# Second layers by seven products of blocks instead of eight, 1024 rows at a time, in channel attention and two MLPs

## Chip, cores and metric

The kernel runs on one core of one Trainium2 chip. The metric is the time on the device in microseconds (us), the median of several runs. For the kernel before it is 1119.35 us, over three runs of 1117.44, 1119.35 and 1119.87 us.

## What is computed

Attention over channels makes a 256 x 256 matrix from q and k and applies it to v; its 6016 rows go through two MLPs of width 2048 one after the other. Cut to what matters:

```python
# q, k, v: 6016 x 256 in fp32; the weights arrive as 64-bit floats
s = (k / (norm(k, axis=1) + 1e-6)).T @ (q / (norm(q, axis=1) + 1e-6)) / tau   # 256 x 256
a = softmax(s)                       # along the last axis
x = v @ a                            # 6016 x 256
h = x @ moe_w_in                     # 6016 x 2048
g = moe_s * maximum(h, 0)**2 + moe_b
y = g @ moe_w_out                    # 6016 x 256
h = y @ moe2_w_in                    # 6016 x 2048
g = maximum(h, 0) + alpha * minimum(h, 0)       # alpha: 2048 values in 0..0.3
out = g @ moe2_w_out                 # 6016 x 256
```

## The kernel before

**Arithmetic.** Every fp32 factor of an MLP is split into a high part (`...h`, the value rounded to the matmul's fp32r type) and a low part (`...l`, what is left), and a product is made of three matmuls: high by high, low weight by high, high weight by low. The attention matrix is folded into the first weights: `w1 = a @ moe_w_in` (four groups `make_w1`, L496 to L509), so x is v itself, turned so that channels lie on partitions.

**Start.** For some 60 us q and k stream in; TensorE makes the score matrix, ACT and DVE the norms and the softmax. Meanwhile and afterwards weights arrive in 32 units of 512 KB and are turned from 64-bit floats into fp32 and split (`unit`): two passes on ACT, four on DVE, then a cast on ACT and a subtraction on DVE.

**Chunks and steps.** The rows are cut into 12 chunks (480, ten of 512, 416). A step `t` is one block of 128 hidden units of one chunk, so there are 12 x 16 = 192 steps. A step has four stages of six matmuls: `stage_a` makes the first MLP's hidden block in a PSUM bank `h1` (L520 to L523, function `hidden`), `stage_b` adds its share to the two output halves `y0`, `y1` (L590 to L592), `stage_c` (bank `h2`, L520 to L523) and `stage_d` (banks `o0`, `o1`, L664 to L666) do the same for the second MLP. `h1` and `h2` have two banks each; with the four for outputs these are the eight banks. Stage B is two steps behind A. The second MLP is a chunk behind the first (`SC = NF + SB`), so from the second chunk on all four stages alternate.

**Around the matmuls.** After stage A ACT makes relu and square (L558, L559), and DVE, in the first chunks ACT, the high part (L537 or L541) and DVE the low part (L542). After stage C ACT makes relu of h and of -h (L633, L634), DVE the multiply-add with alpha (L640) and both parts. At a chunk's end y gets its scale and bias on ACT and is split; the outputs are transposed on DVE (L678) and stored by eight DMAs on SP (L681). The next chunk's v is loaded by SP (`load_v`) and transposed and split by DVE.

**Order.** The instructions of each engine stand in the order in which the code issues them, by hand. A small clock per engine (`run`, `fill`, `PARTS`) decides where the parts of the weight units go between the steps. All DMAs are on SP's queue, except the first pieces of k on ACT's.

## Time and profile before

| | us |
|---|---|
| median of three runs | 1119.35 |
| profiled execution | 1118.72 |
| its span in the profile | 1116.9 |
| PE busy | 1098.7 |
| DVE busy | 740.5 |
| ACT busy | 553.8 |

The granted TensorE clock was 0.996 of full speed over the span. Matmuls overlap in the pipeline: a row of the timeline has a start and a duration, and the next one may start before the first has ended, so the distance between starts, not the duration, is what an instruction takes of its engine. A row ends, in brackets, with the idle time before it and what ended that.

### The profile page before, as it was taken

How to read it: one execution, taken by the hardware profiler on the slowest of the kernel's cores; microseconds unless marked ns; L12 is line 12 of the kernel's file. 1: busy time of each engine (PE TensorE's matmuls, PEld its weight loads, DVE VectorE, ACT ScalarE, POOL GpSimd, SP SyncE). 2: the span in 40 equal slices, each digit the busy share in tenths (PEclk: the TensorE clock that was granted, in tenths of full speed). 3: DMA queues.
4: the chain of work that ended last, by engine and by line, in shares of the span. 5: the costliest groups of instructions: out<-in, count | busy, mean ns of one | idle time of the engine just before them, and what ended most of it. 6: DMA issues, size and time to landing. Idle time of an engine off the chain costs nothing.

```text
span 1116.9 us, 13535 instructions
## 1 busy us (share of the span) xinstructions
PE 1098.7 (98%) x4898; PEld 917.0 (82%) x4898; DVE 740.5 (66%) x1284; ACT 553.8 (50%) x946; POOL 0.7 (0%) x6
## 2 busy tenths in 40 slices
...
PEclk9989999999999999999999999999999999999999
...
DMA packets 114627, 42.31 MB, mean 38 GB/s; under 512 B 102784, under 2 KB 103552, under 8 KB 114560
## 3 DMA queue, kind: packets, MB, share of 16 engines
q1 hardware_dynamic: 113696, 39.35, 14.6%
...
q8 instruction: 38, 0.62, 0.2%
...
## 4 chain that ended last, share of the span: by engine, by line
PE 89%; DVE 7%; DMA 2%; ACT 1%; issue 1%; ACTq 0%; DVEq 0%; SPq 0%
PE h L521 15%; PE h L523 15%; PE h L520 15%; PE o L666 8%; PE o L664 8%; PE o L665 7%; PE y L590 7%; PE y L591 7%; PE y L592 7%; DMA qk<-in_k_dram 2%; DVE acc L353 1%; PE wp L496 1%; DVE g1l L542 0%; DVE sq L340 0%; DVE wi L163 0%
## 5 line engine op out<-in xcount | busy, mean ns | idle before, releaser
L640 DVE SCALAR_TENSOR_TENSOR gc<-neg,nal_sb,gc 128x512 f32<-128x512 f32 (+2 forms) x192 | 141.6, 738 | 178.6 <-ACT neg L634 178.2
L633 ACT ACTIVATE gc<-h 128x512 f32<-128x512 f32 (+2 forms) x192 | 113.1, 589 | 257.7 <-PE h L523 243.1
L558 ACT ACTIVATE ga<-h 128x512 f32<-128x512 f32 (+2 forms) x192 | 113.1, 589 | 252.4 <-PE h L523 233.6
L520 PE MATMUL h<-xh,w1h 128*128 128x512 f32 (+2 forms) x384 | 150.8, 393 | 0.4 <-ACT w1h L505 0.4
L521 PE MATMUL h<-xh,w1l 128*128 128x512 f32 (+2 forms) x384 | 149.4, 389 | 0.2 <-DVE w1l L509 0.2
L590 PE MATMUL y<-g1h,wo1h 128*128 128x512 f32 (+2 forms) x384 | 148.2, 386 | 0.4 <-ACT wo1h L172 0.2
L521 PE MATMUL h<-yh,wi2l 128*128 128x512 f32 (+2 forms) x384 | 148.2, 386 | 0.2 <-DVE wi2l L174 0.2
L591 PE MATMUL y<-g1h,wo1l 128*128 128x512 f32 (+2 forms) x384 | 148.1, 386 | 0.2 <-DVE wo1l L174 0.2
L520 PE MATMUL h<-yh,wi2h 128*128 128x512 f32 (+2 forms) x384 | 147.9, 385 | 0.4 <-ACT wi2h L172 0.4
L592 PE MATMUL y<-g1l,wo1h 128*128 128x512 f32 (+2 forms) x384 | 148.0, 386 | 0.0
L664 PE MATMUL o<-g2h,wo 128*128 128x512 f32 (+2 forms) x368 | 142.7, 388 | 0.5 <-DVE g2h L541 0.5
L666 PE MATMUL o<-g2l,wo 128*128 128x512 f32 (+2 forms) x368 | 142.5, 387 | 0.0
L665 PE MATMUL o<-g2h,wo 128*128 128x512 f32 (+2 forms) x368 | 142.4, 387 | 0.0
L542 DVE TENSOR_TENSOR g1l<-ga,g1h 128x512 fp32r<-128x512 f32 (+2 forms) x192 | 130.7, 681 | 16.8 <-ACT g1h L537 1.9
L542 DVE TENSOR_TENSOR g2l<-gc,g2h 128x512 fp32r<-128x512 f32 (+2 forms) x184 | 126.2, 686 | 17.4 <-PE h L523 0.9
L541 DVE CAST g1h<-ga 128x512 fp32r<-128x512 f32 (+1 forms) x158 | 66.4, 420 | 87.1 <-ACT ga L559 86.0
L559 ACT ACTIVATE ga<-ga 128x512 f32<-128x512 f32 (+2 forms) x192 | 119.7, 623 | 6.1
L523 PE MATMUL h<-xl,w1h 128*128 128x512 f32 (+2 forms) x384 | 117.8, 388 | 0.0
L523 PE MATMUL h<-yl,wi2h 128*128 128x512 f32 (+2 forms) x384 | 116.7, 385 | 0.0
L634 ACT ACTIVATE neg<-h 128x512 f32<-128x512 f32 (+2 forms) x192 | 112.1, 584 | 0.1
L541 DVE CAST g2h<-gc 128x512 fp32r<-128x512 f32 (+2 forms) x184 | 77.9, 423 | 16.9 <-DVE gc L640 0.5
L521 PEld LDWEIGHTS h<-xh,w1l 128*128 128x128 f32 x384 | 72.8, 190 | 15.6 <-issue 1.0
(106 smaller groups left out, 1281.0 us busy)
## 6 DMA issues: line engine op xcount, KB each, us to landing
...
wi1r<-in_moe_w_in_dram SPq DMA_DIRECT2D x8, 512.0 KB, 7.5
wo1r<-in_moe_w_out_dram SPq DMA_DIRECT2D x8, 512.0 KB, 4.3
wi2r<-in_moe_w_in_dram SPq DMA_DIRECT2D x8, 512.0 KB, 3.6
wo2r<-in_moe_w_out_dram SPq DMA_DIRECT2D x8, 512.0 KB, 3.7
...
```

The source lines that it names most:

```text
L520: nc.tensor.matmul(pt[:, :n], wh[:, h, fs], xh, start=(h == 0), stop=False)
L521: nc.tensor.matmul(pt[:, :n], wl[:, h, fs], xh, start=False, stop=False)
L523: nc.tensor.matmul(pt[:, :n], wh[:, h, fs], xhl[h][1][:, :n], start=False, stop=(h == NC2 - 1))
L541: nc.vector.tensor_copy(hi[:, :n], g[:, :n])
L542: nc.vector.tensor_tensor(lo[:, :n], g[:, :n], hi[:, :n].bitcast(F32), ALU.subtract)
L590: nc.tensor.matmul(yp[:, :m], wo1h[:, f, cs], hi[:, :m], start=(f == 0), stop=False)
L591: nc.tensor.matmul(yp[:, :m], wo1l[:, f, cs], hi[:, :m], start=False, stop=False)
L592: nc.tensor.matmul(yp[:, :n], wo1h[:, f, cs], lo[:, :n], start=False, stop=(f == NF - 1))
L640: nc.vector.scalar_tensor_tensor(g[:, :n], neg[:, :n], nal_sb[:, f : f + 1], g[:, :n], op0=ALU.mult, op1=ALU.add,)
L664: nc.tensor.matmul(op, wo2[:, f, 0, cs], hi, start=(f == 0), stop=False)
L665: nc.tensor.matmul(op, wo2[:, f, 1, cs], hi, start=False, stop=False)
L666: nc.tensor.matmul(op, wo2[:, f, 0, cs], lo, start=False, stop=(f == NF - 1))
```

## The change

**Seven products.** Rows are taken 1024 at a time, as two halves: six chunks of 2 x 480, 2 x 512 (four) and 2 x 480 rows. The unit is now a *cycle* c, one pair of hidden blocks (256 units) of one chunk: 8 pairs x 6 chunks x 2 MLPs = 96 cycles. A cycle makes four hidden tiles by the first layer, as before with six matmuls each (`a_tile`, i: hidden block i % 2, half i // 2): B11, B21 of the first half, B12, B22 of the second. The second layer multiplies a 2 x 2 scheme of weight blocks (A) with these four by Strassen's scheme in Winograd's form: seven products, each of three matmuls into a bank of its own, P1 to P7, where the sum over the eight pairs is kept. Before, this took eight products. The sums of blocks on the data side, `T1 = B12 - B11`, `B12 = B22 - B12`, `B11 = B12 + B11`, `B21 = B21 - B11`, are made by DVE in fp32, then split into high and low parts G0 to G3 (`g_ops`); those on the weight side are made once for each unit. The seven banks are put together at the end of each chunk by additions on DVE (`results`). With seven banks for the products, one is left, `h`, for all hidden tiles.

**Order of the MLPs.** All six chunks go through the first MLP (cycles 0 to 47), then all through the second (48 to 95). The results of the first go to DRAM (`yd`) by DMAs on POOL's queue and are read back as the second's input, into a ring of three slots `xt`. The second MLP's weight units are converted and split during the first half, staged in DRAM (`wid`, `wod`) and read back into the first's places around cycles 40 to 48, on POOL's queue too.

**Steps of the activations.** In the first half ACT makes relu from the bank and then squares. In the second, ACT copies the tile out of the bank with a scale per partition of +1 or -1 (`sg_sb`, the sign folded into the weights), and DVE makes max(g * alpha, g) in one instruction (L700).

**Who sets the order.** A class `Plan` now collects all instructions behind the start with their engine, an estimated duration, and what they read and write, and sorts them by a list schedule: TensorE's order is as written, ACT's and DVE's go by the latest start time, and a cast may go to either engine. `LOOK` keeps ACT free shortly before a tile's bank is to be emptied (`boost` over 5).

```diff
-        chunks.append((n0, min(CH if n0 else CH - 32, N - n0)))
+    sizes = [480, 512, 512, 512, 512, 480]
+    firsts = [2 * sum(sizes[:j]) for j in range(len(sizes))]
+    NCHUNK = len(sizes)
...
-        bufs = 2 if tag in ("h1", "h2") else 1
-        return ps.tile([P, CH], F32, tag=tag, name=name, bufs=bufs)
+        return ps.tile([P, CH], F32, tag=tag, name=name)
...
+BACKLOG = (0.8, 3.0)
+LOOK = 0.2
...
+            for o in now:
+                us = o["us"][e] if isinstance(o["us"], dict) else o["us"]
+                if any(u["boost"] > 5 and u["r"] < t + us - look.get(e, 9.0) for u in soon):
+                    continue
+                pick = o
+                break
+            if pick is None:
...
+        parts += [
+            ("dve", est("tt", P), lambda: sub(S[:, 0, :], A21, A22, ALU.add), [kw], [ks]),
+            ("dve", est("tt", P), lambda: sub(S[:, 1, :], S[:, 0, :], A11, ALU.subtract), [kw], [ks]),
+            ("dve", est("tt", P), lambda: sub(S[:, 2, :], A11, A21, ALU.subtract), [kw], [ks]),
+            ("dve", est("tt", P), lambda: sub(S[:, 3, :], A12, S[:, 1, :], ALU.subtract), [kw], [ks]),
...
+        PROD = {
+            "P1": (0, 0, 0), "P2": (2, 0, 1), "P3": (6, 1, 0), "P5": (3, 2, 0),
+            "P7": (5, 2, 1), "P6": (4, 3, 0), "P4": (1, 3, 1),
+        }
...
+        def a_tile(c, i):
+            ph, j, p = c // 48, c // 8 % NCHUNK, c % 8
+            n = sizes[j]
+            f2, x = i % 2, i // 2
+            kx = (2 * (c // 8) + x) % 3
+            qq, f0 = p // 2, (p % 2) * 2 + f2
+            def go():
+                t = hb[c, i] = bank("h", f"h{c}_{i}")
+                w, xx = W["wA", qq], xt[kx]
+                fs = slice(f0 * P, (f0 + 1) * P)
+                for h in range(NC2):
+                    nc.tensor.matmul(t[:, :n], w[:, h, 0, fs], xx[:, h, 0, :n], start=(h == 0), stop=False)
+                    nc.tensor.matmul(t[:, :n], w[:, h, 1, fs], xx[:, h, 0, :n], start=False, stop=False)
+                for h in range(NC2):
+                    nc.tensor.matmul(t[:, :n], w[:, h, 0, fs], xx[:, h, 1, :n], start=False, stop=(h == NC2 - 1))
+            reads = [("x", kx, h, y) for h in range(2) for y in range(2)]
+            reads += [("wAh", qq, h) for h in range(2)] + [("wAl", qq, h) for h in range(2)]
+            op("pe", 6 * (0.0133 + n * 0.2134 / CH), go, reads, [("bank", "h")])
+            g = gA[c % 2][:, f2, :n] if x == 0 else gB[:, 1 + f2, :n]
+            kg = ("gA", c % 2, f2) if x == 0 else ("gB", 1 + f2)
+            if ph == 0:
+                op("act", est("act", n), lambda: nc.scalar.activation(g, hb.pop((c, i))[:, :n], AF.Relu),
+                   [("bank", "h")], [kg], boost=6.0)
+            else:
+                fc = 2 * p + f2
+                op("act", est("act", n), lambda: nc.scalar.activation(
+                    g, hb.pop((c, i))[:, :n], AF.Copy, scale=sg_sb[:, fc : fc + 1]),
...
+        def g_ops(c):
+            ph, j, p = c // 48, c // 8 % NCHUNK, c % 8
+            n = sizes[j]
+            a = gA[c % 2]
+            k11, k21, kt, k12, k22 = ("gA", c % 2, 0), ("gA", c % 2, 1), ("gB", 0), ("gB", 1), ("gB", 2)
+            V = nc.vector
+            B11, B21, T1, B12, B22 = a[:, 0, :n], a[:, 1, :n], *(gB[:, i, :n] for i in range(3))
+            if ph == 0:
+                op("act", est("act", 2 * n), lambda: nc.scalar.activation(
+                    a[:, :, :n], a[:, :, :n], AF.Square), [], [k11, k21])
+                for g, kk in ((B12, k12), (B22, k22)):
+                    op("act", est("act", n), lambda g=g: nc.scalar.activation(g, g, AF.Square), [], [kk])
+            else:
+                for f2, g, kk in ((0, B11, k11), (1, B21, k21), (0, B12, k12), (1, B22, k22)):
+                    al = al_sb[:, 2 * p + f2 : 2 * p + f2 + 1]
+                    op("dve", est("stt", n), lambda g=g, al=al: V.scalar_tensor_tensor(
+                        g, g, al, g, op0=ALU.mult, op1=ALU.max), [], [kk])
+            def hilo(k, src, keys):
+                m = len(keys)
+                hi, lo = (G[k][:, y, :m, :n] if m > 1 else G[k][:, y, 0, :n] for y in (0, 1))
+                kh = [("Gh", k, x) for x in range(m)]
+                kl = [("Gl", k, x) for x in range(m)]
+                op(either, HI(m * n), lambda e: copy(e, hi, src), keys, kh, leave=BACKLOG[ph])
+                op("dve", est("tt", m * n), lambda: V.tensor_tensor(
+                    lo, src, hi.bitcast(F32), ALU.subtract), keys + kh, kl)
+            tt = est("tt", n)
+            hilo(0, a[:, :, :n], [k11, k21])
+            op("dve", tt, lambda: V.tensor_tensor(T1, B12, B11, ALU.subtract), [k11, k12], [kt])
+            op("dve", tt, lambda: V.tensor_tensor(B12, B22, B12, ALU.subtract), [k22], [k12])
+            hilo(1, B22, [k22])
+            op("dve", tt, lambda: V.tensor_tensor(B11, B12, B11, ALU.add), [k12], [k11])
+            op("dve", tt, lambda: V.tensor_tensor(B21, B21, B11, ALU.subtract), [k11], [k21])
+            hilo(2, gB[:, 0:2, :n], [kt, k12])
+            hilo(3, a[:, :, :n], [k11, k21])
...
+        def b_mms(c):
+            j, p = c // 8 % NCHUNK, c % 8
+            n = sizes[j]
+            first, last = p == 0, p == NPAIR - 1
+            res = []
+            for tag, (wb, k, x) in PROD.items():
+                m = n + 2 if c < 8 and tag in ("P1", "P2", "P5") else n
+                for s in range(3):
+                    def go(tag=tag, wb=wb, k=k, x=x, s=s, m=m):
+                        if first and s == 0:
+                            acc_t[tag] = bank(tag, f"{tag}_{c}")
+                        w = W["wB", p]
+                        cols = m if s < 2 else n
+                        nc.tensor.matmul(
+                            acc_t[tag][:, :cols], w[:, int(s == 1), wb, :],
+                            G[k][:, int(s == 2), x, :cols],
+                            start=(first and s == 0), stop=(last and s == 2),
+                        )
+                    half = 1 if wb >= 3 else 0
+                    kw = ("wBl" if s == 1 else "wBh", p) + ((1,) if half else ())
+                    res.append((go, [kw, ("Gl" if s == 2 else "Gh", k, x)], [("bank", tag)], 0.0133 + n * 0.2134 / CH))
+            return res
...
+            keep(1, "P1", m)
+            if ph:
+                keep(P2, "P2")
+            add(0, 1, P2, m)
+            keep(4, "P3")
...
+            if ph:
+                keep(P7, "P7")
+                keep(P6, "P6")
+                keep(P4, "P4")
+            add(1, 1, P6)
+            add(2, 1, P7)
+            add(1, 1, 3)
+            add(3, 2, 3)
+            add(4, 1, 4)
+            add(2, 2, P4)
...
+                op("sp", 0.7, lambda: nc.gpsimd.dma_start(xt[k][:, :, :, :n], yd[2 * j + x][:, :, :, :n]),
+                   [("yd", j, x, h) for h in range(2)] + late,
+                   [("x", k, h, y) for h in range(2) for y in range(2)], late=6.0)
...
+        NCYC = 2 * NCHUNK * NPAIR
+        W1_AT = {1: (1, ("P6", "P4")), 3: (2, ("h", "h")), 5: (3, ("h", "h"))}
+        for c in range(NCYC + 1):
...
+                users = [lambda i=i: a_tile(c, i) for i in range(4)]
...
+            bs = b_mms(c - 1) if c else []
+            nb = 0
+            for i, u in enumerate(users):
+                u()
+                upto = len(bs) * (i + 1) // len(users)
+                while nb < upto:
+                    g, r, w, us = bs[nb]
+                    op("pe", us, g, r, w)
+                    nb += 1
...
+            if c < NCYC:
+                g_ops(c)
+            if c % 8 == 0 and c:
+                results(c // 8 - 1)
...
+            if 40 <= c <= 48:
+                p = c - 41
+                if p >= 0:
+                    op("sp", 0.7, lambda p=p: nc.gpsimd.dma_start(W["wB", p], W["wod"][p]),
+                       [("wod", p)], [(x, p, *y) for x in ("wBh", "wBl") for y in ((), (1,))], late=6.0)
...
+        for o in pl.schedule({"act": LOOK, "dve": 0.5}, {"act": 0.5, "dve": 1.0}):
+            if len(o["eng"]) > 1:
+                o["fn"](o["by"])
+            else:
+                o["fn"]()
...
-        SB = 2
-        SC = NF + SB
-        SD = SC + 1
-                finish_a.append(stage_a(t, on_act))
-                stage_b(t - SB)
-                finish_c = stage_c(t - SC)
-                    stage_d(d)
```

**TensorE's order in the middle.** Before, around step 103: `h2_87` is the hidden tile of the second MLP, `o5_0` and `o5_1` its outputs; the numbers behind `yh`, `g2h` and `wi2h` are the buffers'.

```order
L520 MATMUL h2_87_5089<-yh5_0_4717,wi2h_866 128x512
L521 MATMUL h2_87_5089<-yh5_0_4717,wi2l_867 128x512
L520 MATMUL h2_87_5089<-yh5_1_4721,wi2h_866 128x512
L521 MATMUL h2_87_5089<-yh5_1_4721,wi2l_867 128x512
L523 MATMUL h2_87_5089<-yl5_0_4718,wi2h_866 128x512
L523 MATMUL h2_87_5089<-yl5_1_4722,wi2h_866 128x512
L664 MATMUL o5_0_4841<-g2h86_1_5058,wo2_868 128x512
L665 MATMUL o5_0_4841<-g2h86_1_5058,wo2_868 128x512
L666 MATMUL o5_0_4841<-g2l86_1_5059,wo2_868 128x512
L664 MATMUL o5_1_4842<-g2h86_1_5058,wo2_868 128x512
L665 MATMUL o5_1_4842<-g2h86_1_5058,wo2_868 128x512
L666 MATMUL o5_1_4842<-g2l86_1_5059,wo2_868 128x512
```

After, in cycle 75: `h75_2` and `h75_3` are its third and fourth tile, `P5_72` and the like the banks of the chunk that began with cycle 72, filled from G0 to G3 of cycle 74; `x2` and `x3` are repetitions of a row.

```order
L666 MATMUL h75_3_6533<-x1_98,wA1_409 128x512
L667 MATMUL h75_3_6533<-x1_98,wA1_409 128x512
L666 MATMUL h75_3_6533<-x1_98,wA1_409 128x512
L667 MATMUL h75_3_6533<-x1_98,wA1_409 128x512
L669 MATMUL h75_3_6533<-x1_98,wA1_409 128x512 x2
L738 MATMUL P6_72_6394<-G3_427,wB2_414 128x512 x3
L738 MATMUL P4_72_6400<-G3_427,wB2_414 128x512 x3
L666 MATMUL h76_0_6551<-x0_97,wA2_410 128x512
L667 MATMUL h76_0_6551<-x0_97,wA2_410 128x512
L666 MATMUL h76_0_6551<-x0_97,wA2_410 128x512
L667 MATMUL h76_0_6551<-x0_97,wA2_410 128x512
L669 MATMUL h76_0_6551<-x0_97,wA2_410 128x512 x2
```

Six product matmuls (five, five, five and six of the 21 follow the four tiles) now stand between two tiles that use the same bank, where before six matmuls of a tile alternated with six of an output and the tiles took turns in two banks.

**DVE's order in the middle.** Before, one step: the multiply-add of the second MLP, its high and low part, and the two parts of the first MLP's block.

```order
L640 SCALAR_TENSOR_TENSOR gc82_4877<-neg82_4878,nal_sb_68,gc82_4877 128x512
L541 CAST g2h82_1_4881<-gc82_4877 128x512
L542 TENSOR_TENSOR g2l82_1_4882<-gc82_4877,g2h82_1_4881 128x512
L541 CAST g1h101_1_4904<-ga101_4901 128x512
L542 TENSOR_TENSOR g1l101_1_4905<-ga101_4901,g1h101_1_4904 128x512
```

After, one cycle of the second half: `gA0`, `gA1` hold B11 and B21 of this cycle and the next in turn, `gB` holds T1, B12 and B22; L716 to L720 are the sums.

```order
L700 SCALAR_TENSOR_TENSOR gA1_422<-gA1_422,al_sb_69 128x512
L700 SCALAR_TENSOR_TENSOR gB_423<-gB_423,al_sb_69 128x512
L716 TENSOR_TENSOR gB_423<-gB_423,gA1_422 128x512
L709 TENSOR_TENSOR G0_424<-gA1_422,G0_424 128x1024
L700 SCALAR_TENSOR_TENSOR gB_423<-gB_423,al_sb_69 128x512
L717 TENSOR_TENSOR gB_423<-gB_423 128x512
L709 TENSOR_TENSOR G1_425<-gB_423,G1_425 128x512
L719 TENSOR_TENSOR gA1_422<-gB_423,gA1_422 128x512
L720 TENSOR_TENSOR gA1_422<-gA1_422 128x512
L709 TENSOR_TENSOR G2_426<-gB_423,G2_426 128x1024
L700 SCALAR_TENSOR_TENSOR gA0_421<-gA0_421,al_sb_69 128x512
L709 TENSOR_TENSOR G3_427<-gA1_422,G3_427 128x1024
```

The casts to the high parts have left DVE here, the sums have come, and low parts of two blocks are one instruction of 1024 columns.

**DVE's order at the end.** Before, behind the last multiply-add:

```order
L640 SCALAR_TENSOR_TENSOR gc191_9374<-neg191_9375,nal_sb_68,gc191_9374 128x416
L541 CAST g1h191_2_9378<-gc191_9374 128x416
L542 TENSOR_TENSOR g1l191_2_9379<-gc191_9374,g1h191_2_9378 128x416
L678 STREAM_TRANSPOSE ot11_0_9401<-o11_0_9092 128x416
L678 STREAM_TRANSPOSE ot11_1_9407<-o11_1_9093 128x416
```

After, from the last low part on; `cb0` to `cb3`, `wf2`, `raw0` and `raw1` hold the banks' contents, L769 are the additions and L819 the transposes:

```order
L709 TENSOR_TENSOR G3_427<-gA1_422,G3_427 128x2x480
L819 STREAM_TRANSPOSE yo0_1019<-cb0_428 128x480
L769 TENSOR_TENSOR cb1_429<-cb1_429,cb2_430 128x480
L769 TENSOR_TENSOR cb2_430<-cb1_429,raw0_75 128x480
L769 TENSOR_TENSOR cb1_429<-cb1_429,cb3_431 128x480
L769 TENSOR_TENSOR cb3_431<-cb2_430,cb3_431 128x480
L769 TENSOR_TENSOR wf2_80<-cb1_429,wf2_80 128x480
L769 TENSOR_TENSOR cb2_430<-cb2_430,raw1_76 128x480
L819 STREAM_TRANSPOSE yo1_1020<-wf2_80 128x480
L819 STREAM_TRANSPOSE yo0_1019<-cb3_431 128x480
L819 STREAM_TRANSPOSE yo1_1020<-cb2_430 128x480
```

Before, the transposes read the output banks directly; now six additions of copies lie between the last products and three of the four transposes.

## Rows read from the trace of the kernel before

**Rows 1.** The page: span; busy time per engine; the granted clock in slices

```profile
span 1116.9 us, 13535 instructions
...
PE 1098.7 (98%) x4898; PEld 917.0 (82%) x4898; DVE 740.5 (66%) x1284; ACT 553.8 (50%) x946; POOL 0.7 (0%) x6
...
PEclk9989999999999999999999999999999999999999
```

**Rows 2.** Stretches: start:end, length, PE, PEld, DVE, ACT, POOL busy, clock, DMA, GB/s

```profile
60.00:80.00 20.00, 17.47 (x46) 10.45 (x46) 17.68 (x39) 14.96 (x26) 0.00 (x0) 0.83 0.34 105
80.00:100.00 20.00, 19.85 (x84) 15.15 (x82) 19.47 (x45) 19.53 (x36) 0.00 (x0) 1.00 0.43 106
...
500.00:600.00 100.00, 100.00 (x442) 82.80 (x442) 61.87 (x105) 43.50 (x76) 0.00 (x0) 1.00 0.07 11
```

**Rows 3.** Timeline of PE: start, duration, engine, line, operation, tile, shape; two stretches

```profile
81.39 0.38 PE L520 MATMUL h<-xh,w1h 128*128 128x480 f32 x1
...
82.69 0.38 PE L590 MATMUL y<-g1h,wo1h 128*128 128x482 f32 x1
...
500.27 0.39 PE L520 MATMUL h<-xh,w1h 128*128 128x512 f32 x1
...
505.71 0.39 PE L520 MATMUL h<-xh,w1h 128*128 128x512 f32 x1
```

**Rows 4.** Timeline of PE, two neighbours between 60 and 80 us

```profile
68.37 0.60 PE L520 MATMUL h<-xh,w1h 128*128 128x480 f32 x1
68.77 0.60 PE L521 MATMUL h<-xh,w1l 128*128 128x480 f32 x1
```

**Rows 5.** Timeline of PE and ACT: from a tile's last matmul to ACT and back

```profile
65.26 0.69 ACT L505 ACTIVATE w1h<-wp,rinv 128x512 fp32r<-128x512 f32 x1 [1.63 <-PE wp L496]
...
66.00 0.77 PE L520 MATMUL h<-xh,w1h 128*128 128x480 f32 x1 [0.35 <-ACT w1h L505]
...
501.18 0.62 PE L523 MATMUL h<-xl,w1h 128*128 128x512 f32 x2
...
501.83 0.60 ACT L558 ACTIVATE ga<-h 128x512 f32<-128x512 f32 x1 [1.63 <-PE h L523]
...
504.55 0.60 ACT L633 ACTIVATE gc<-h 128x512 f32<-128x512 f32 x1 [1.46 <-PE h L523]
505.04 0.59 ACT L634 ACTIVATE neg<-h 128x512 f32<-128x512 f32 x1
```

**Rows 6.** Groups by shape: line, operation, tiles, count | busy, mean ns | idle before

```profile
L542 DVE TENSOR_TENSOR g1l<-ga,g1h 128x512 fp32r<-128x512 f32 x160 | 110.8, 692 | 14.6 <-ACT g1h L537 1.2 <-DVE g1h L541 0.5
...
L640 DVE SCALAR_TENSOR_TENSOR gc<-neg,nal_sb,gc 128x512 f32<-128x512 f32 x160 | 119.8, 749 | 170.8 <-ACT neg L634 170.6
...
L353 DVE TENSOR_TENSOR acc<-acc,sq 128x2560 f32<-128x2560 f32 x6 | 16.9, 2823 | 17.3 <-ACT sq L351 17.2
...
L505 ACT ACTIVATE w1h<-wp,rinv 128x512 fp32r<-128x512 f32 x8 | 5.5, 684 | 4.9 <-PE wp L496 4.8
```

**Rows 7.** Timeline of DVE: neighbours with and without something to wait for

```profile
80.29 0.74 DVE L509 SCALAR_TENSOR_TENSOR w1l<-wp,rinv,w1h 128x512 fp32r<-128x512 f32 x1
80.95 0.65 DVE L542 TENSOR_TENSOR g1l<-ga,g1h 128x480 fp32r<-128x480 f32 x1
81.52 0.16 DVE L570 CAST g1h<-ones 128x2 fp32r<-128x2 f32 x1
...
500.23 0.75 DVE L640 SCALAR_TENSOR_TENSOR gc<-neg,nal_sb,gc 128x512 f32<-128x512 f32 x1 [1.32 <-ACT neg L634]
501.08 0.43 DVE L541 CAST g2h<-gc 128x512 fp32r<-128x512 f32 x1
```

**Rows 8.** Timeline of the end: the last matmul and the last stores

```profile
1110.17 0.35 PE L666 MATMUL o<-g1l,wo 128*128 128x416 f32 x1
...
1110.64 4.02 SPq L681 DMA_DIRECT2D out_dram<-ot  x8
```

**Rows 9.** DMA issues: tile, queue, count, KB each, median us to landing

```profile
wi2r<-in_moe_w_in_dram SPq DMA_DIRECT2D x8, 512.0 KB, 3.6
```

869 lines of the change are left out of this document (456 added, 413 removed).

## The prediction

> **What bounds the kernel now.** I read the page first, then the stretches, then the timeline of single steps. The page gives 1116.9 us of span, PE busy for 98% of it, DVE for 66% and ACT for 50%, and a granted clock of nine tenths of full speed or more in all slices but the third [rows 1]. The stretches say where: from 60 to 80 us PE ran 17.5 of 20 us at a granted clock of 0.83, and from 500 to 600 us it was busy 100 of 100 us while DVE had 62 and ACT 44 [rows 2]. So after a start of some 130 us nothing but the number and pitch of matmuls sets the time. The timeline gives the pitch. One step of 24 matmuls of 512 columns runs from 500.27 to 505.71, so 5.44 / 24 = 0.2267 us each; six of 480 columns take 81.39 to 82.69, so 0.2167 us [rows 3]. A page's rule speaks against this reading: the Trainium skill (Trainium Kernel Development and Optimization, Performance Expectations) says that matmul busy time is a bad measure because matmuls are pipelined, and that the busy share of LDWEIGHTS is a good one. That share is 82% here, so by the rule PE would have room and fewer matmuls might give nothing. The even starts, 0.2267 us apart with nothing waited for, decide against it; what is left of it is a rival below.
>
> **What is removed.** Before, each 128 x n block of hidden units takes 6 matmuls in each of four layers: 192 x 24 = 4608. After, a cycle (a pair of hidden blocks, two halves of n rows) takes four first-layer tiles of 6 and seven products of 3, so 45 instead of 48, and there are 96 cycles: 4320. With 16 x 24 = 384 matmuls per chunk, before costs 384 x (0.2167 + 10 x 0.2267 + 0.188 for the chunk of 416) = 1025.9 us. After has 32 cycles of 480 columns at 45 x 0.2167 = 9.75 us and 64 of 512 at 10.2 us: 312.0 + 652.9 = 964.9 us. PE loses **61.0 us**. This is the whole gain, and it lies on the path, since PE has no idle time to give.
>
> **The start.** The prelude up to the score matrix is the same code, and w1 still needs its two first unit conversions, so the first tile again gets going at about 66.0 us, where the tile of before waited for ACT [rows 5]. The other three groups of w1 matmuls cost 10.7 us as before. New: in cycle 0 there are no products yet to put between the tiles, and all tiles share one PSUM bank, so each waits for ACT to empty it: about 0.7 us a tile (from the end of a tile to the release, below), 2.8 us. Matmuls after the first waits came 0.40 us apart, half the clock [rows 4]; I charge 3 us for that. PE alone would end at 66.0 + 964.9 + 10.7 + 2.8 + 3.0 = 1047.4 us.
>
> **The bank of the tiles.** Before, h1 and h2 have two banks each; after, one bank for all first-layer tiles, because seven hold the products. Cover is the 5 or 6 product matmuls between two tiles. ACT starts 0.03 us after the tile's last matmul ends (501.18 + 0.62, ACT at 501.83) and takes 0.60 us; PE went on 0.05 us after ACT had released it (65.26 + 0.69, PE at 66.00) [rows 5]. From the last matmul's start this is 0.39 + 0.03 + 0.60 + 0.05 = 1.07 us; the next tile is due 6 x 0.2267 = 1.36 us after that start. So ACT may be 0.29 us late. In the second half the tile is emptied with a scale per partition, and that form took 0.684 us [rows 6], which leaves 0.20 us. I cost this at nothing: ACT carries a pitch sum of some 228 of 245 us in cycles 8 to 31 (independent ones start 0.49 us apart [rows 5]) and 5.3 to 8.3 us of a cycle later, and the order keeps long casts off the moments at which tiles end. If the cover goes, it is the slower rival.
>
> **DVE is the new neighbour of the bound.** The blocks' sums are its work. Before, a step of 5.44 us holds one multiply-add, two casts and two subtractions. After, a cycle of the second half holds four multiply-max, four sums and four subtractions of low parts, three of them of 1024 columns; casts go to ACT. What an instruction occupies is its duration less 0.08 us (0.74 starts 0.66 after, 0.65 starts 0.57 after [rows 7]): 0.61 for a sum or subtraction of 512 (0.692 long), 0.66 for a multiply-max (0.749), 1.14 for 1024 columns (on the line between 0.692 for 512 and 2.823 for 2560) [rows 6]. A 512 cycle is 4 x 0.66 + 4 x 0.61 + 3 x 1.14 + 0.61 = 9.1 us, and the results of a chunk (seven sums, four transposes) add 6.8 / 8 = 0.85: 9.95 of PE's 10.2 us. Summed over the order of the changed kernel by these pitches: 104 us in cycles 0 to 7 (eight units of weights now also get four block sums and seven blocks to split), 243 in 8 to 31, 124 in 32 to 47, 470 in 48 to 95. PE's shares are 88, 244.8, 159.6 and 482.4. So DVE is 118%, 99%, 78% and 97% of PE.
>
> What that costs has no row; I bound it. *Lower*: DVE runs packed from 64 us. Cycle 31's last low part is then ready at 64 + 347 = 411, and PE ends cycle 32 at 411.9 against 410.8 alone: 1 us, and nothing later. *Upper*: where DVE was full before it did not run packed. Between 80 and 200 us (without 120 to 140) its instructions by the same pitches sum to 93.6 of 100 us, in stretches like the one of 80 to 100 [rows 2]. At 0.936 the first part needs 370.6 us and costs 25, and the last 48 cycles need 502 against 482.4, 20 more: 45 us. *Between*: an instruction that reads the one before it starts about 0.1 us later than its duration less 0.08 lets expect (500.23 to 501.08 behind 0.749 [rows 7]); some 50 such neighbours up to cycle 31 and some 100 from 48 on give 7 + 4 = 11 us over PE. I take **18**, nearer to the neighbours than to the old rate, since the order puts other work between most of them, but with some waits for ACT's casts.
>
> **The tail.** Before, 6.4 us lie between the last matmuls and the end: two transposes, eight stores issued in 4.02 us, landing [rows 8]. After, the last cycle's blocks must be formed after the last tile (about 6.1 us of DVE, of which 4.6 are covered by products), and the last two products are followed by six sums and three transposes, 5.5 us, then four stores of 0.5 and 2 us of landing: 11.2 us behind PE's ideal end.
>
> **Moves on the queues.** Results of the first half go to DRAM and come back, and the second half's weights are reloaded, all on POOL's queue, which had no DMA before. A load of 1 MB for the second half's rows may take from the end of tile 1 of a chunk's last cycle to tile 2 of the next, 11.3 us; 512 KB landed in 3.6 us [rows 9], so twice that is 7.2. Hidden; if each were 5 us longer than that rather than hidden, five chunk starts would lose some 1 us each, and this is in the range.
>
> **Sum.** 1047.4 + 18 + 11.2 = 1076.6 us of span. The profiled execution lies 1.8 us above its span (1118.72 against 1116.9), and the median of the three runs 0.6 above that: **1079 us**, 40 less than 1119.35.
>
> **Rivals.** *DVE's order hides nearly all* (e at 1 to 6): 1061 to 1066. For it: sums that are just under PE's; against: the first 32 cycles are at 101% with weights. *DVE sets the pace* at its old rate: 1106. For it: 97 and 99% leave nothing for a wait, and both engines are in order. *Slower than before*: the tiles' bank. 384 tiles; with 1061 us without such waits, a mean wait of 58 / 384 = 0.15 us makes it even, and 0.2 us gives 1138. It decides once ACT starts 0.29 + 0.15 us late on the mean, that is, if one tile in two meets a cast of 1 us half done. For it: ACT at 93% in the first half; against: the order leaves ACT idle before many tiles. Such short waits could also cost clock, as from 60 to 80 us, where waits of 0.2 to 0.4 us stood ahead of the 0.40 us pitch [rows 2, 4]: a cycle at half the clock costs 45 x 0.18 = 8 us more, and seven or eight of 96 eat the gain. The Trainium skill (TensorE: Matmul & The Clock Gate, A second HAM failure mode: psum-queue depth-cycling) describes this, PE idling briefly between groups while PSUM is cycled, and the clock going back and forth; here the clock was full wherever PE did not wait, and only the start shows it reduced. *No change*: matmuls were not the bound, and 0 us come of 61: about 1121.
>
> **How the numbers follow.** Forecast, 1066 to 1092: 0.58. All hidden, below 1066: 0.14. DVE's pace, 1092 to 1112: 0.18. Within 0.2% of before (what a measurement can tell): 0.02. Slower by the bank or the clock: 0.08. Range 1060 to 1105: it leaves out the slow cases and the end of DVE's pace. Faster 0.90, same 0.02, slower 0.08.
>
> **What would show it.** Matmuls 0.2267 us apart inside a tile and inside a group of products, 4320 of them: else the first term is wrong. PE's waits: on DVE (G low parts) some 20 us in total, mostly before 420 us and just behind the chunk starts of the second half; on ACT for h, a few us. DVE busy above 90% outside cycles 32 to 47. Granted clock 1.00 after 85 us. If PE waits for ACT's emptying of h more than for DVE, the bank is the cause; if a chunk of 512 in the second half takes over 85 us with DVE full, DVE sets the pace. If POOL's loads end last anywhere, my reading of the queue is wrong.

## The result, and the profile after

The changed kernel takes 1125.12 us (median of nine runs, 1121.29 to 1129.36) against 1118.47 us for the kernel before (nine runs, 1116.31 to 1119.87). The ratio is 1.0067, with a 95% interval of 1.0047 to 1.0087: slower by 0.7%, where 1079 us and a range of 1060 to 1105 had been forecast.

The page of the changed kernel, the same three rows as in [rows 1]:

```profile
span 1121.1 us, 13090 instructions
...
PE 1063.2 (95%) x4610; PEld 853.3 (76%) x4610; DVE 1008.7 (90%) x1454; ACT 816.5 (73%) x1168; POOL 39.8 (4%) x70
...
PEclk9999999999999999999999999999999999999998
```

PE has 288 matmuls less, 4898 against 4610, but it is no longer always busy: 95% of the span in place of 98%, while DVE went from 66% to 90% and ACT from 50% to 73%. In this execution, of 1122.91 us, the clock is not what was lost: its mean granted clock is 0.991, against 0.996 before, and one of the few short stretches at half the clock is shown below. Over the nine runs the granted clock goes from 0.991, at 1121.29 us, down to 0.982, at 1129.36 us, so the spread among them follows the clock.

Where the time is can be read off the first tile of a cycle. The rows are PE's L669 matmuls (the fifth and sixth of a tile) at the first tile of cycles 0, 8, 32, 48, 56, 88 and 95:

```profile
67.00 0.60 PE L669 MATMUL h<-x,wA 128*128 128x480 f32 x2
...
165.85 0.63 PE L669 MATMUL h<-x,wA 128*128 128x512 f32 x2
...
424.87 0.62 PE L669 MATMUL h<-x,wA 128*128 128x512 f32 x2
...
590.35 0.59 PE L669 MATMUL h<-x,wA 128*128 128x480 f32 x2
...
679.57 0.62 PE L669 MATMUL h<-x,wA 128*128 128x512 f32 x2
...
1022.03 0.59 PE L669 MATMUL h<-x,wA 128*128 128x480 f32 x2
...
1092.31 0.59 PE L669 MATMUL h<-x,wA 128*128 128x480 f32 x2
```

Against them stands what the matmuls alone need at 0.2267 and 0.2167 us: 24 for the tiles of each cycle of a stretch and 21 for the products of each cycle one earlier, in cycles 0 to 7 also the 10.7 us of w1.

| cycles | length, us | matmuls alone | lost |
|---|---|---|---|
| 0 to 7 | 98.9 | 84.2 | 14.7 |
| 8 to 31 | 259.0 | 244.6 | 14.4 |
| 32 to 47 | 165.5 | 159.8 | 5.7 |
| 48 to 55 | 89.2 | 78.0 | 11.2 |
| 56 to 87 | 342.5 | 326.2 | 16.2 |
| 88 to 94 | 70.3 | 68.5 | 1.8 |

Together 64.0 us are lost between the tiles, in every stretch, where the prediction had 23.8 (5.8 at the start and 18 for DVE); behind the last mark and the matmuls still due from there (62 x 0.2167 us) lie 15.4 us, where 11.2 had been summed behind PE's ideal end. Busy times in the same stretches (columns as in [rows 2]):

```profile
165.80:424.90 259.10, 250.51 (x1082) 201.02 (x1082) 245.71 (x377) 232.25 (x356) 16.70 (x26) 1.00 0.36 100
...
679.60:1022.00 342.40, 336.10 (x1441) 266.72 (x1440) 324.64 (x429) 214.79 (x285) 4.16 (x7) 1.00 0.16 37
```

DVE is busy for 95% of both. In the first of them ACT has 90%, in the second only 63%. So in the second stretch DVE looks like the bound, but not quite: what it waits for there (waits of DVE: engine, line, waited for: us in total, times, longest us) is ACT's emptying of the tiles,

```profile
DVE gB L700 <- ACT gB L681: 11.7, 12, 1.1
DVE G L709 <- ACT G L359: 2.8, 11, 0.5
```

and PE waits, over the whole span, partly for ACT's emptying (L677, L681), partly for DVE:

```profile
PE h L666 <- ACT gA L677: 11.9, 21, 1.5
PE P L738 <- DVE cb L769: 10.6, 5, 5.8
PE P L738 <- DVE G L709: 4.9, 10, 2.0
```

For the whole span DVE's first wait, L700 on gB for L681, adds up to 18.4 us.

An ordinary cycle of the second half, away from chunk starts, is the plainest place. PE and ACT around 736 us (timeline; start, duration):

```profile
735.54 0.61 PE L669 MATMUL h<-x,wA 128*128 128x512 f32 x2
735.99 1.29 PE L738 MATMUL P<-G,wB 128*128 128x512 f32 x5
737.41 0.50 PE L666 MATMUL h<-x,wA 128*128 128x512 f32 x1
...
735.00 1.78 ACT L359 CAST G<-gB 128x512 fp32r<-128x512 f32 x2 [0.83 <-DVE gB L700]
736.68 0.68 ACT L681 ACTIVATE gA<-h,sg_sb 128x512 f32<-128x512 f32 x1
```

The tile's last matmul ends at 736.15. ACT could empty the bank then, but it is within its second cast, the one of 1024 columns, and empties from 736.68 to 737.36. PE's five products are due to end at 735.99 + 5 x 0.2267 = 737.12; the next tile begins at 737.41 and starts slowly. From the tile at 735.54 to that of the cycle after, at 746.23, are 10.69 us, where 45 x 0.2267 is 10.20. In 16 of the 32 cycles from 56 to 87 the first tile is emptied more than 0.2 us late like this, in cycles 8 to 31 in 20 of 24. Summed over all tiles, the first matmul behind an emptying that began over 0.2 us late comes some 23 us later than the pitch allows. The list of waits has only 15.2 us for ACT's emptying (11.9 and three smaller lines), since a PE row's modelled duration reaches over short gaps.

A chunk start, on PE and then on DVE, around the longest wait:

```profile
608.48 1.20 PE L738 MATMUL P<-G,wB 128*128 128x480 f32 x3
615.44 1.57 PE L738 MATMUL P<-G,wB 128*128 128x480 f32 x3 [5.76 <-DVE cb L769]
616.81 0.60 PE L666 MATMUL h<-x,wA 128*128 128x480 f32 x1
617.21 0.60 PE L667 MATMUL h<-x,wA 128*128 128x480 f32 x1
...
614.74 0.65 DVE L769 TENSOR_TENSOR cb<-cb,P 128x480 f32<-128x480 f32 x1
```

The first product P4 of a new chunk waits until DVE has added up the old one, which it does at 614.74, behind all the sums of the cycle. After the 5.76 us the matmuls are 0.40 us apart for a while, half the clock (granted clock 0.83 over these 20 us):

```profile
600.00:620.00 20.00, 14.12 (x55) 11.34 (x54) 18.45 (x28) 11.87 (x16) 2.69 (x4) 0.83 0.34 101
```

The end, which answers to [rows 8]:

```profile
1105.22 2.78 PE L738 MATMUL P<-G,wB 128*128 128x480 f32 x10 [0.97 <-DVE G L709]
...
1112.36 1.20 DVE L819 STREAM_TRANSPOSE yo<-cb 128x480 f32<-128x480 f32 x2
...
1107.42 11.32 SPq L826 DMA_DIRECT2D out_dram<-yo  x16
```

### The profile page after: what moved, and what is told of

Read it like the earlier page. It is cut to its first block, busy times and chain, and to the rows that moved or that the text cites. A ratio compares the mean times of both kernels' runs of the same rounds, so it can differ in the third digit from the quotient of the medians.

```text
span 1121.1 us, 13090 instructions
## 1 busy us (share of the span) xinstructions
PE 1063.2 (95%) x4610; PEld 853.3 (76%) x4610; DVE 1008.7 (90%) x1454; ACT 816.5 (73%) x1168; POOL 39.8 (4%) x70
## 3 DMA queue, kind: packets, MB, share of 16 engines
q1 hardware_dynamic: 113696, 39.35, 14.4%
## 4 chain that ended last, share of the span: by engine, by line
PE 60%; DVE 17%; ACT 15%; issue 4%; DMA 3%; ACTq 0%; DVEq 0%; SPq 0%
PE P L738 24%; PE h L666 12%; PE h L669 11%; PE h L667 11%; DVE G L709 6%; ACT G L359 5%; DMA qk<-in_k_dram 3%; DVE gB L700 3%; DVE gB L717 2%; ACT gA L681 2%; ACT gB L681 1%; ACT gB L677 1%; ACT gA L677 1%; PE wp L619 1%; ACT gB L696 1%
## 5 line engine op out<-in xcount | busy, mean ns | idle before, releaser
L738 PE MATMUL P<-G,wB 128*128 128x512 f32 (+2 forms) x2016 | 523.2, 389 | 18.3 <-DVE cb L769 10.6
L738 PEld LDWEIGHTS P<-G,wB 128*128 128x128 f32 x2016 | 377.6, 188 | 101.5 <-DVE cb L769 12.8
L666 PE MATMUL h<-x,wA 128*128 128x512 f32 (+1 forms) x768 | 305.6, 398 | 17.8 <-ACT gA L677 11.9
L667 PE MATMUL h<-x,wA 128*128 128x512 f32 (+1 forms) x768 | 298.2, 388 | 0.3 <-DVE wA L633 0.3
L709 DVE TENSOR_TENSOR G<-gA,G 128x1024 fp32r<-128x1024 f32 (+1 forms) x192 | 229.4, 1197 | 40.5 <-ACT G L359 40.1
L669 PE MATMUL h<-x,wA 128*128 128x512 f32 (+1 forms) x768 | 234.7, 387 | 0.0
L359 ACT CAST G<-gA 128x1024 fp32r<-128x1024 f32 (+1 forms) x189 | 193.7, 1027 | 27.7 <-DVE gA L720 19.0
L666 PEld LDWEIGHTS h<-x,wA 128*128 128x128 f32 x768 | 144.2, 188 | 78.8 <-ACT gA L677 25.9
L359 ACT CAST G<-gB 128x512 fp32r<-128x512 f32 (+1 forms) x192 | 156.9, 821 | 49.8 <-DVE gB L700 41.4
L709 DVE TENSOR_TENSOR G<-gB,G 128x512 fp32r<-128x512 f32 (+1 forms) x192 | 179.2, 937 | 1.5 <-ACT G L359 1.1
L669 PEld LDWEIGHTS h<-x,wA 128*128 128x128 f32 x768 | 144.4, 188 | 28.7
L667 PEld LDWEIGHTS h<-x,wA 128*128 128x128 f32 x768 | 144.6, 188 | 23.4 <-DVE wA L633 0.6
L681 ACT ACTIVATE gB<-h,sg_sb 128x512 f32<-128x512 f32 (+1 forms) x96 | 65.3, 681 | 76.6 <-PE h L669 76.4
L681 ACT ACTIVATE gA<-h,sg_sb 128x512 f32<-128x512 f32 (+1 forms) x96 | 65.1, 678 | 46.0 <-PE h L669 45.8
L700 DVE SCALAR_TENSOR_TENSOR gB<-gB,al_sb 128x512 f32<-128x512 f32 (+1 forms) x96 | 70.6, 735 | 18.7 <-ACT gB L681 18.4
L677 ACT ACTIVATE gA<-h 128x512 f32<-128x512 f32 (+1 forms) x96 | 56.3, 587 | 28.9 <-PE h L669 28.6
L700 DVE SCALAR_TENSOR_TENSOR gA<-gA,al_sb 128x512 f32<-128x512 f32 (+1 forms) x96 | 70.6, 735 | 4.5 <-ACT gA L681 4.0
L677 ACT ACTIVATE gB<-h 128x512 f32<-128x512 f32 (+1 forms) x96 | 56.5, 588 | 24.8 <-PE h L669 24.3
L716 DVE TENSOR_TENSOR gB<-gB,gA 128x512 f32<-128x512 f32 (+1 forms) x96 | 64.8, 676 | 1.4 <-ACT gB L696 0.6
L720 DVE TENSOR_TENSOR gA<-gA 128x512 f32<-128x512 f32 (+1 forms) x96 | 64.9, 676 | 1.2
## 6 DMA issues: line engine op xcount, KB each, us to landing
qk<-in_q_dram SPq DMA_DIRECT2D x7, 640.0 KB, 10.6
```

The costliest lines, as they stand in the source:

```text
L359: nc.scalar.copy(o, i)
L666: nc.tensor.matmul(t[:, :n], w[:, h, 0, fs], xx[:, h, 0, :n], start=(h == 0), stop=False)
L667: nc.tensor.matmul(t[:, :n], w[:, h, 1, fs], xx[:, h, 0, :n], start=False, stop=False)
L669: nc.tensor.matmul(t[:, :n], w[:, h, 0, fs], xx[:, h, 1, :n], start=False, stop=(h == NC2 - 1))
L677: op("act", est("act", n), lambda: nc.scalar.activation(g, hb.pop((c, i))[:, :n], AF.Relu), [("bank", "h")], [kg], boost=6.0)
L681: op("act", est("act", n), lambda: nc.scalar.activation(g, hb.pop((c, i))[:, :n], AF.Copy, scale=sg_sb[:, fc : fc + 1]), [("bank", "h")], ...
```

## Experiments

Eleven variants of the changed kernel ran, beside runs of the kernel before on the same chip. For each, the table has the ratio to the kernel before with its interval; *chunk* is the time from cycle 64 to 72 (matmuls alone 81.6 us), *ordinary* the usual length of a cycle away from chunk starts (alone 10.20 us; marks as in the list above). Every edit goes through the planner, which then makes a new order for ACT and DVE as a whole; no run holds the rest of the order fixed, so a difference of a few us between two variants can be the planner's.

| variant | us | ratio (95%) | chunk | ordinary |
|---|---|---|---|---|
| the change | 1125.12 | 1.0067 (1.0047 to 1.0087) | 84.7 | 10.7 |
| d1 second bank for tiles | 1128.71 | 1.0094 (1.0071 to 1.0117) | 87.3 | 10.20 |
| d2 no sums | 1076.75 | 0.962 (0.9592 to 0.9647) | 81.9 | 10.2 |
| d3 no additions | 1121.65 | 1.0019 (1.0004 to 1.0033) | 86.3 | 10.65 |
| d4 eight products | 1119.09 | 1.0008 (0.9999 to 1.0017) | | |
| d5 = d1 + d3 | 1082.36 | 0.9683 (0.9669 to 0.9697) | 82.2 | 10.20 |
| e2 one sum less | 1120.23 | 1.0025 (1.0011 to 1.0039) | 85.2 | 10.67 |
| e3 one sum on POOL | 1167.76 | 1.0449 (1.0423 to 1.0475) | 90.7 | 11.3 |
| e6 LOOK -0.4 | 1149.96 | 1.0298 (1.0259 to 1.0336) | 89.4 | 10.7 |
| f1 emptying first | 1106.16 | 0.9902 (0.9885 to 0.9919) | 83.0 | 10.2 |
| g1 = f1 + d3 | 1082.56 | 0.968 (0.9666 to 0.9694) | 82.3 | 10.2 |
| f3 = f1 + chunk starts, end | 1092.16 | 0.9768 (0.9749 to 0.9787) | 82.9 | 10.2 |

**First four: which of the three is it?** The theories were the tiles' one bank, DVE's sums, and the additions at a chunk's end; a fourth run asked whether the new order costs anything without Strassen.

d1, two banks for the tiles:

```diff
-                t = hb[c, i] = bank("h", f"h{c}_{i}")
+                t = hb[c, i] = bank(HB[i % 2], f"h{c}_{i}")
...
-                        if first and s == 0:
+                        if tag == "P4":
+                            acc_t[tag] = acc_t["P6"]
+                        elif first and s == 0:
```

> The seventh product P4 is accumulated into the bank of P6 (which leaves out nothing of the work, but makes the outputs wrong), and its bank becomes a second one for the hidden tiles. Theory BANK (the tiles' single bank costs the time, about 12 us of waits for ACT gA/gB before tiles and as much again in slow first matmuls behind such waits, 5 to 8 us more hidden in chunk starts): 1090 to 1100 us, and no wait of PE for ACT's emptying of h is left. Theory DVE (the four sums per cycle fill DVE, and PE goes at DVE's pace): no more than 5 us come back, 1118 to 1125, and waits for G's low parts take the place of those for ACT.

It took 1128.7 us, above both expectations: the theory that the bank alone costs the time fell. But not one wait for the emptying is left in its ordinary cycles, which run at exactly 10.20 us; the time is lost at chunk starts, where cycle 65, for one, takes 15.0 us and PE waits for G's low parts (waits of PE in d1, and of DVE):

```profile
PE P L742 <- DVE G L711: 16.4, 15, 2.2
...
DVE gB L702 <- ACT gB L683: 17.2, 28, 0.9
```

The second bank takes away PE's waits for a late emptying, but not DVE's: 17.2 us here, 18.4 in the change. Two things are mixed into the time. The granted clock was 0.974 to 0.980 in d1's four executions, against 0.982 to 0.991 in the change; from the two means, 0.977 and 0.986, I estimate some 10 us of PE's time. And the bank that P6 and P4 share is needed one product earlier at a chunk start than P4's own was; what that costs has no run.

d2, no block sums:

```diff
-            op("dve", tt, lambda: V.tensor_tensor(T1, B12, B11, ALU.subtract), [k11, k12], [kt])
-            op("dve", tt, lambda: V.tensor_tensor(B12, B22, B12, ALU.subtract), [k22], [k12])
-            op("dve", tt, lambda: V.tensor_tensor(B11, B12, B11, ALU.add), [k12], [k11])
-            op("dve", tt, lambda: V.tensor_tensor(B21, B21, B11, ALU.subtract), [k11], [k21])
-            hilo(2, gB[:, 0:2, :n], [kt, k12])
+            hilo(2, gB[:, 1:3, :n], [k12, k22])
```

> The four sums of blocks per cycle (L716, L717, L719, L720) are left out, and the products read the blocks as they are: DVE has 2.4 us less in each of 96 cycles, everything else is issued as before. Theory DVE: DVE falls to some 75% of PE's time, its waits go, 1070 to 1080 us. Theory BANK: the sums are not what PE waits for; the casts on ACT still meet the tiles' ends, 1105 to 1120 us.

1076.75 us: as the theory of DVE had it. PE's waits for DVE and ACT fall to a few us while DVE now waits 121 us for ACT's casts and nobody minds (a wait of PE, a wait of DVE):

```profile
PE P L734 <- DVE G L709: 2.2, 3, 0.8
...
DVE G L709 <- ACT G L359: 120.7, 109, 4.2
```

So one bank is enough for tiles as long as the sums are not there.

d3, no additions: the seven `add` lines of `results` are left out and P2 and P7 copied in their place. Nothing reads P6 and P4 any more, so ACT's copies of these two go as well.

> The seven additions at the end of a chunk are left out; four of the seven banks are copied and go out as they are. Theory RESULTS (at a chunk's start the first products wait until DVE has added the old banks up: 10.6 us of waits for cb and what follows them): 1105 to 1112 us, with no wait for cb of more than 1 us, and the tail 5 us shorter. Theory DVE: the same waits move to G's low parts, since seven additions are 4 us of some 85 in a chunk: 1113 to 1120 us, nearly all of it from the tail. Theory BANK: as DVE.

1121.65 us, above all three expectations and nearest to those of DVE and the bank. The waits for cb are gone, and yet the chunk takes 86.3 us: its ordinary cycles take 10.65 as before, while DVE's waits for the emptying of gB rose from 18.4 to 37.0 us. So DVE's sum of work cannot be the whole reason: 36 us less of it (1008.7 to 972.3 busy) gave 3.5.

d4, eight products into four banks in the same order:

```diff
-            "P1": (0, 0, 0), "P2": (2, 0, 1), "P3": (6, 1, 0), "P5": (3, 2, 0),
-            "P7": (5, 2, 1), "P6": (4, 3, 0), "P4": (1, 3, 1),
+            ("P1", 1, 0, 0), ("P1", 3, 0, 1), ("P5", 0, 0, 0), ("P5", 2, 0, 1),
+            ("P2", 1, 2, 0), ("P2", 3, 2, 1), ("P3", 0, 2, 0), ("P3", 2, 2, 1),
```

> Chunks of 1024 rows, the order of the two MLPs, the reloads on POOL's queue and the planner stay, but the second layers take the usual eight products into four banks: no sums of blocks, no additions at a chunk's end, two banks for the tiles, 48 matmuls a cycle. Matmuls alone: 66 + 32 x 48 x 0.2167 + 64 x 48 x 0.2267 + 10.7 = 1106 us, tail 8. If the loss is in what the seven products add (sums, additions, the single bank): 1115 to 1122 us, about the kernel before. If chunks, phases or POOL's queue cost something by themselves: 1130 or more.

1119.09 us, the time of the kernel before, with PE busy 98%, as the page shows:

```profile
PE 1100.7 (98%) x4898; PEld 916.9 (82%) x4898; DVE 555.6 (50%) x711; ACT 676.5 (61%) x951; POOL 41.5 (4%) x70
```

Chunks of 1024 rows, the two phases, POOL's queue and the planner cost nothing measurable where DVE has room (50% busy). All of the loss is in what the seven products bring with them. That holds for the start too: cycles 0 to 7 lose 2.8 us in d4, but 13.4 in d2 and 12.4 in d5 below, so leaving out the sums of a cycle (d2) or the one bank and the additions (d5) keeps most of that loss, if some of d2's is the clock, as in f3 below. The weights' own sums and seven blocks, which only d4 leaves out, are the likely cause, but no run leaves out these alone.

**Second four: two limits of the same height?** d1 and d3 together suggested that: in an ordinary cycle the one bank holds PE, at a chunk start DVE's work does, and each alone gives the same time.

> Both earlier edits at once: two banks for the tiles (P4 accumulated into P6's bank) and no additions at a chunk's end. Alone they gave 1128.7 and 1121.7 us. Theory TWO LIMITS (in an ordinary cycle the one bank holds PE at 10.65 us, and over a chunk DVE's whole work holds it at some 85 us; taking one away leaves the other): now both are away, a chunk of 512 in the second half takes 82 to 83 us instead of 85 to 86, and the whole 1085 to 1098 us. Theory DVE ALONE (the sum of DVE's work is the only limit): as with no additions alone, 1115 to 1122 us.

1082.36 us, 3 below the range of TWO LIMITS, and a chunk of 82.2: the two edits gain next to nothing one by one (+3.6 and -3.5 us) and 42.8 us together. That DVE alone is the limit is refuted. That there are two limits is shown; that both must go before anything is gained is not, as f1 below gains with the additions in place.

e2 left out the last sum alone (L720):

> One of the four sums of a cycle is left out (L720, the last of the chain): DVE has 0.6 us less per cycle, 58 us in all. Theory DVE ALONE: what goes from DVE comes back from the time until PE is the limit: 1078 to 1090 us. Theory TWO LIMITS: the waits at chunk starts go (some 20 us), the meeting of ACT's casts with the tiles' ends in ordinary cycles stays (0.4 us a cycle): 1095 to 1110 us.

1120.23 us, neither theory's number. The waits for cb fell from 10.6 to 6.0 us, but the ordinary cycles stayed at 10.67; I had overrated what the chunk starts were worth while the ordinary cycles were held. It speaks once more against DVE's total: its busy time fell from 1008.7 to 965.2 us, and that gave 5.

e3 put T1 on POOL, `nc.gpsimd.tensor_tensor` for `V.tensor_tensor` in L716:

> The sum T1 = B12 - B11 of every cycle is computed on POOL instead of DVE (nothing is left out). DVE has 0.6 us less per cycle as with one sum less; POOL's time for it is in no trace so far, the planner is told 1.2 us. Theory DVE ALONE: 1080 to 1095 us. Theory TWO LIMITS: 1095 to 1112 us. If POOL takes over 3 us for it, or slows DVE down while it runs, no gain or a loss: 1120 us or more.

1167.76 us, the last of its three cases; what POOL does to DVE is in the last section.

e6, `LOOK = -0.4`:

> One number: LOOK from 0.2 to -0.4, so ACT begins no cast that by the plan ends later than 0.4 us before a tile has to be emptied (before: up to 0.2 us after). Nothing is left out. Theory TWO LIMITS: ordinary cycles fall to PE's pace, 10.2 us, as with two banks, and chunk starts get longer, because DVE's work is the same: 1118 to 1128 us. If the bank is the only limit: 1090 to 1100 us. If casts that come later keep DVE waiting in every cycle: 1130 us or more.

1149.96 us, as the last of its three cases: ordinary cycles stayed at 10.7, and the third cycle of a chunk in the second half rose to 13 to 15 (14.8 in cycle 66, 10.8 in the change). In cycles 56 to 87 the first tile of 24 was now emptied over 0.2 us late, not of 16. Keeping ACT clear for longer did not bring the emptying forward. That sent me to the planner's choice itself. It keeps ACT idle ahead of a tile's end, but when the end comes, a cast and the emptying are both ready, and among ready instructions the earlier latest start decides; in the ordinary cycle that was the cast of 1024 columns. The two casts in a row ahead of L681, above, are this choice.

**Last three: the order as the cause.** f1 changes the choice alone:

```diff
-            now = sorted((o for o in c if o["r"] <= t), key=lambda o: (o["lst"], o["i"]))
+            now = sorted((o for o in c if o["r"] <= t), key=lambda o: (o["boost"] <= 5, o["lst"], o["i"]))
```

> One rule of the planner, nothing of the work: where the emptying of a tile's bank and a cast are both ready on ACT, the emptying goes first (before, the one with the earlier latest start went first, which in ordinary cycles was the cast of 1024 columns). Theory TWO LIMITS with the order of the planner as the cause of the first: ordinary cycles go from 10.67 to 10.2 us with one bank, as with two; DVE has slack there, so unlike with LOOK the casts come in time; chunk starts keep some of their waits: 1085 to 1095 us. If the single bank itself is too tight (0.2 us of slack in the second half, whatever the order): ordinary cycles stay above 10.5 and the whole above 1110 us. If DVE's total work is the limit after all, chunk starts take what the ordinary cycles give, as with two banks: 1118 to 1128 us.

1106.16 us, 19 less than the change and 1% faster than the kernel before, with one bank and all sums; in time that lies between its three cases, in ordinary cycles it is TWO LIMITS. The same place in f1, PE and ACT:

```profile
742.64 0.61 PE L669 MATMUL h<-x,wA 128*128 128x512 f32 x2
743.09 1.30 PE L738 MATMUL P<-G,wB 128*128 128x512 f32 x5
744.23 0.40 PE L666 MATMUL h<-x,wA 128*128 128x512 f32 x1
...
742.08 0.62 ACT L359 CAST G<-gB 128x512 fp32r<-128x512 f32 x1 [0.82 <-DVE gB L700]
743.35 0.69 ACT L681 ACTIVATE gA<-h,sg_sb 128x512 f32<-128x512 f32 x1 [0.65 <-PE h L669]
743.93 1.04 ACT L359 CAST G<-gB 128x1024 fp32r<-128x1024 f32 x1
```

The cast of 1024 columns now stands behind the emptying, which begins 0.10 us after the tile's end (742.64 + 0.61) instead of 0.53; the next tile starts when the products are done, 743.09 + 5 x 0.2267 = 744.22. Cycles 56 to 87 fell from 342.5 to 332.2 us, and the first matmuls behind a late emptying now come 3 us late in all, not 23. DVE's waits for the emptying went as well, which the second bank of d1 had left (waits of DVE, of the change, then of f1):

```profile
DVE gB L700 <- ACT gB L681: 18.4, 20, 1.1
...
DVE gB L700 <- ACT gB L681: 5.5, 17, 0.3
```

So the late emptying held two engines, PE by the bank and DVE by its input; d1 freed only the first. The gain is smaller than I had expected, since chunk starts kept their waits for cb (13.3 us).

> The same rule and, as in an earlier run, no additions at a chunk's end (four of the seven banks are copied and go out as they are). Theory TWO LIMITS: with the rule in the place of the second bank this comes to the same as two banks without additions, 1082 us: 1072 to 1088. If the rule does not do what the second bank did: 1105 us or more.

1082.56 us, the time of d5: without additions, and where the emptying goes first, the second bank has nothing left to give. Against f1 the additions, with the copies of P6 and P4, are worth 23.6 us now; some 4.5 of these lie behind the last tiles (28.8 us from cycle 95's mark to the end in f1, 24.3 in g1).

f3 adds to f1 what the chunk starts and the end seemed to need; the last line also takes the planner's `look` for DVE from 0.5 to 0.2, which the expectation does not name:

```diff
-                   boost=2.0 if isinstance(b, str) else 0.0)
+                   boost=4.9 if isinstance(b, str) else 0.0)
...
+            own = ph or cc == NCHUNK - 1
+            P2, P6, P7, P4 = (0, 2, 5, 6) if own else ("P2", "P6", "P7", "P4")
...
+                            (nc.scalar if cc == 11 and g % 2 else nc.sync).dma_start(
...
-                    add_unit(n, after=(n - 16) * 19.0 + 100.0)
+                    add_unit(n, after=(n - 16) * 20.0 + 110.0)
...
-        for o in pl.schedule({"act": LOOK, "dve": 0.5}, {"act": 0.5, "dve": 1.0}):
+        for o in pl.schedule({"act": LOOK, "dve": 0.2}, {"act": 0.5, "dve": 1.0}):
```

> The rule, and for the chunk starts and the end: additions that free a bank come earlier (boost 4.9 in place of 2); the last chunk of the first half is copied out of its banks by ACT as in the second half; weight units of the second MLP start 10 us later and 20 us apart; half of the last chunk's stores go out on ACT's queue. Nothing is left out. TWO LIMITS: 12 us less than the rule alone by fewer waits at chunk starts (the 5.8 us of the first chunk of the second half among them), and 3 us at the end, which had 12 stores one after the other at 0.47 us: 1070 to 1082 us. If DVE's work at chunk starts only moves: no more than the 3 us of the end, 1083 to 1092 us.

1092.16 us, 2.3% faster than the kernel before and the fastest that computes everything. The stretches of f3 for cycles 8 to 31, 48 to 55 and 56 to 87:

```profile
169.40:417.10 247.70, 245.92 (x1082) 202.08 (x1082) 240.46 (x368) 220.74 (x336) 14.50 (x23) 1.00 0.34 94
...
580.40:659.70 79.30, 78.85 (x362) 66.30 (x361) 77.01 (x108) 54.82 (x78) 4.64 (x8) 1.00 0.26 89
659.70:991.90 332.20, 329.76 (x1442) 266.36 (x1441) 324.25 (x429) 213.27 (x284) 4.13 (x7) 1.00 0.16 38
```

They lose 3.0, 1.3 and 6.0 us now, in place of 14.4, 11.2 and 16.2, and no wait for cb is left above 1 us. It missed its expectation by 10 us all the same and came out at the upper edge of the other case. Splitting the stores gave less than 1 us of the 3: from the last transpose's end to the end of the span are 6.8 us against 7.5, since the six stores that stand behind the last transposes on ACT's queue took 4.43 us. And cycle 8 begins 3.6 us later than in the change. Most of that is the clock (the stretch from 67 to 82 us, of the change, then of f3; the last but two is the granted clock):

```profile
67.00:82.00 15.00, 10.25 (x41) 7.12 (x40) 14.36 (x30) 13.39 (x23) 0.00 (x0) 1.00 0.34 105
...
67.00:82.00 15.00, 12.91 (x32) 9.30 (x33) 9.97 (x20) 8.69 (x15) 0.00 (x0) 0.54 0.31 105
```

In both, PE waits for ACT between the four tiles of cycle 0, which have no products between them. In f3 the clock is at its lower level, 1.2 GHz, right behind such a wait, and 26 matmuls start 0.40 us apart in place of 0.2167, some 5 us; cycles 0 to 7 take 5.4 us longer than in the change, where the clock was full in this stretch. Why it falls in one of the two and not in the other, no run shows. The 1.2 us for which PE waits for x in cycle 8 come on top, and I have not explained them. What is left is mostly in cycles 0 to 7, 20.2 us, those 5 among them.

## Why the prediction was wrong

**What is removed: right.** 4320 matmuls of MLP layers at 0.2267 and 0.2167 us each are there, and where nothing waits, a cycle takes 10.20 us; d2 shows what that is worth. The Trainium skill (Trainium Kernel Development and Optimization, Performance Expectations) calls the busy share of weight loads a good metric for how close a kernel is to the roofline. Read as room on PE, it misleads here: the share is 82% in the kernel before and in d4, where PE had nothing to give, and a cut of the matmuls was worth its full time in d2.

**The bank of the tiles: the step that failed.** "I cost this at nothing", with 0.20 us of reserve in the second half, because "the order keeps long casts off the moments at which tiles end". The reserve was right, the order did not do that: 58 of the 384 tiles were emptied later than the reserve (0.29 us in the first half, 0.20 in the second), in ordinary cycles by some 0.5 us, where the planner puts a cast of 1024 columns first. I took the purpose of `LOOK` for its effect; the order of the changed kernel on ACT, which I had, shows two casts in a row ahead of an L681, and the choice among ready instructions stands in the code. f1 shows that this one rule is worth 19 us. The rival named the mechanism ("meets a cast of 1 us half done") and asked for one tile in two; it was about one in seven, and what carried the time past that of the kernel before came from the terms below. That the change came out slower, as this rival had it with 0.08, is therefore only in part its doing. The signs on record did not decide between bank and DVE: PE waited 15.2 us for the emptying against 15.5 for DVE, and a chunk of 512 took 84.7 us where 85 was the mark.

**DVE: the sums were right, the price was not.** DVE was occupied 247 us in cycles 8 to 31 (length less its waits) where 243 had been summed. But I priced DVE and the bank one by one, as if the worse of them decided. They are coupled: DVE's multiply-max waits for the emptying (11.7 us in cycles 56 to 87), so a late emptying takes from DVE the 0.25 us of a cycle by which it is faster than PE (9.95 of 10.2). d1 and d3 give next to nothing alone and 43 us together. That a late DVE in turn makes casts come late and meet tiles fits d2, where DVE has room and, with the old rule, 21 tiles are emptied over 0.2 us late and not 71, but no run shows it by itself. One reading behind the 18 us was wrong as well: from 500.23 to 501.08 are 0.85 us where the pitch lets 0.67 expect, so the later start is 0.18 us, not 0.1; and 7 + 4 does not follow from either with the numbers of neighbours given.

**Chunk starts: the second step that failed.** I spread the additions evenly over the chunk (0.85 us a cycle), so their burst cost nothing in the sum. They come close together, with banks waiting for them, and the parts G0 to G3 have one buffer each, so that nothing absorbs the burst: 10.6 us of waits for cb, 5.76 of them at once, and half the clock behind these. With the order mended, leaving out the additions gave 23.6 us (g1 against f1), some 19 of them ahead of the tail. That is as much as the bank.

**The start and the tail: too small.** 14.7 us in cycles 0 to 7 against 5.8; 15.4 us at the end against 11.2, for three transposes free twelve stores, not four, which SP issues one after the other, some 0.5 us apart, until 1118.74.

**Queues: right.** No wait of PE for a reload stands in the list of the change; x of 1 MB landed in 5.1 us, below the 7.2 that I had taken.
